# Routed attention and a bilinear feed-forward layer: weights rounded in pairs of chunks through one raw room, and a sum reloaded in front of the last down product

## The chip, the cores and the metric

One core of a Trainium2 chip. The time is the device time of one execution in microseconds (us), the median of several runs; less is better.

## The reference

```python
q_assign = argmax(q_n @ c_n, -1); k_assign = argmax(k_n @ c_n, -1)    # 16 clusters
mask = q_assign[..., :, None] == k_assign[..., None, :]
scores = where(mask, q @ k.T / sqrt(64), -1e9)
x = softmax(scores) @ v            # B=4, H=8, S=768, D=64; x becomes (3072, 512)
out = ((x @ w_a) * (x @ w_b)) @ w_out    # w_a, w_b: 512 x 1536, w_out: 1536 x 512, fp32
```

A query attends only to the keys of its own cluster. The three weights come as float64.

## The kernel before, in words

The sixteen pairs of heads of the four batches are worked one after the other. The first five are **dense**: scores of blocks of S x S (L599, keys of another cluster masked by a product of one-hot rows), exponentials on ACT (L612), products with v (L641), sums of the exponentials on DVE (`acc`, L630), denominators (L661), and a normalisation on DVE into `xT` (L681 to L694). The other eleven are **sorted**: rows are put into buckets of clusters by indirect DMAs of POOL (L1518), reloaded from DRAM (L1548 into `sq` and `sk`, L1552 into `v`), turned (L1561), scored and multiplied with v inside their buckets only (L1584 to L1619), normalised (L1629), kept (L1641) and fetched back in token order (L1652). The preparation of a sorted pair assigns clusters and counts places on DVE: copies L1384 (ACT) and L1408, then L1413 to L1506.

As soon as a batch's `xT` is ready, its feed-forward pieces follow on PE (helper line L734 for all their matmuls). Batch 0 does its ups plainly, in two halves of tokens (`ffn_block`: a product with w_a copied to `ha` at L787, a product with w_b multiplied into `h` at L791). Batches 1 to 3 use a scheme of seven products for ups (`ffn_ups`) and downs (`ffn_downs`, L1068 adds the products into `ha`, `rest` and `comb`, from which L761 stores the output). The sums of weights S1 to S4 that `ffn_ups` needs are computed in batch 1, kept in DRAM (`up_sums`) and reloaded later (L871 for S1 to S3, L880 for S4). S1's slot is `comb`, the same room that a down product's result lies in until it is stored.

**The weights.** float64 is rounded to fp32 by hand, in 36 chunks of 128 x 512. `load_w` (L306) brings a chunk of 512 KB of 8-byte words into one of two rooms `raw`. `round_w` does five DVE operations right behind each other (L317, L320, L324, L327, L335; `rest` is a room of its own) and a test of the exponents on ACT (L331, L332). Chunks 0 to 7 stand in fixed groups of the dense stage; the others come when `next_round` sees DVE idle by the planner's clock, or on demand: `up` rounds what its column block still lacks before it issues its product, w_a and w_b alternately.

**What sets the order.** The program is written out by a planner that keeps a clock per engine, runs each pair's chain of steps when its condition holds and fills PE with feed-forward pieces. Every engine executes its instructions in the order written; SP issues nearly all the DMAs, also in order, and stands at a DMA whose inputs are not there.

Of the kernel before, what the change touches and what calls it, by code (L numbers as in the profile page):

```python
# [157 lines left out]
def short_path(nc, tc, ctx, c, cn, centroids_in, casts, n_far, q, k, v,  # L158
# [20 lines left out]
    V, Vs, Vc, Vh, Vm, Vl, Vd, Vd_ = (Clocked(nc.vector, "V", us, *state)  # L179
                                      for us in (0.56, 0.19, 0.29, 0.44, 0.7, 0.83, 0.96, 0.42))  # L180
    S_, Ss, Sl = (Clocked(nc.scalar, "S", us, *state) for us in (0.5, 0.3, 0.85))
    Gi = Clocked(nc.gpsimd, "G", 1.28, *state)
    Qs = Clocked(nc.scalar, "S", 0.1, *state)
    Q_, Qr, Qc = (Clocked(nc.sync, "P", us, *state) for us in (0.42, 0.62, 2.0))
# [111 lines left out]
    def weight_room(i):  # L296
        if not deep or (i - deep[0]) % 4 > 1:
            return rawp.tile([P, WN], INT64, name="raw")
        at_ = (i - deep[0]) % 4 * 2 * WN
        return R_["wide"][:, at_:at_ + 2 * WN].bitcast(INT64)  # L300

    def load_w(i):
        if i >= len(w_parts):
            return
        raw = weight_room(i)
        Q_.dma_start(out=raw, in_=w_parts[i][1])  # L306
        raws[i] = raw

    def round_w(i):
        w = w_parts[i][0]  # L310
        wi = w.bitcast(INT32)
        raw = raws.pop(i)
        halves = lambda dt: raw.bitcast(dt).rearrange("p (n two) -> p n two", two=2)
        lo, hi = halves(UINT32)[:, :, 0], halves(INT32)[:, :, 1]


        Vh.tensor_scalar(out=wi, in0=hi, scalar1=3, scalar2=0x3FFFFFF8,  # L317
                                op0=ALU.logical_shift_left,
                                op1=ALU.bitwise_and)
        Vm.scalar_tensor_tensor(out=wi, in0=hi, scalar=SIGN_TOP, in1=wi,  # L320
                                       op0=ALU.bitwise_and, op1=ALU.bitwise_or)
# [5 lines left out]
        Vm.scalar_tensor_tensor(out=rest, in0=lo, scalar=2.0 ** -52,  # L327
                                       in1=rest, op0=ALU.mult, op1=ALU.mult)

        size = sizep.tile([P, WN], FP32, name="size")  # L330
        S_.activation(out=size, in_=halves(FP32)[:, :, 1], func=AF.Abs)  # L331
        S_.activation(out=size, in_=size, func=AF.Relu, scale=-STEEP,  # L332
                      bias=steep[:, 0:1],
                      accum_out=stat[:, 4 * NPAIR + i:4 * NPAIR + i + 1])
        V.tensor_tensor(out=w, in0=w, in1=rest, op=ALU.add)  # L335
# [421 lines left out]

    def store_next():
# [49 lines left out]
    def room():  # L808
        if not W:
            W["raw"] = [rawp.tile([P, 2 * WN], FP32, name="raw") for _ in range(2)]  # L810
            W["size"] = [sizep.tile([P, WN], FP32, name="size") for _ in range(2)]
# [27 lines left out]
    def ffn_ups(b, h):  # L839
# [158 lines left out]
        return pieces, both(*parts[0][0][1:3])  # L998
# [223 lines left out]
    def late_room():  # L1222
# [13 lines left out]
        R_.update(sq=sq, sk=sk, sqT=sqT, skT=sq, O=sqT, v=new(20 * (D + 1)))  # L1236
# [5 lines left out]
        loaded(deep[0] + 1)  # L1242
# [1006 lines left out]
```

## Time and profile before

| | |
|---|---|
| median of 3 runs | 936.36 us (936.02 to 937.34) |
| the profiled execution | 936.02 us |
| its span, first to last instruction | 934.2 us |
| mean granted clock of TensorE | 0.997 |
| PE busy | 916.4 us (98%) |
| DVE busy | 595.6 us (64%) |
| ACT busy | 252.1 us (27%) |
| POOL busy | 403.6 us (43%) |

The profiled execution's own time is its span and 1.8 us around it. The span holds matmuls from about 1 us to 928 us. Shares are means over the whole program; DVE's 64% is far from even, as the windows below show.

### The profile page before, as it was taken

The numbers are of one execution on the slowest core, as the hardware profiler recorded it, in microseconds if no ns is written. First come the engines' busy times: TensorE is split into PE (matmuls) and PEld (weight loads), VectorE is DVE, ScalarE is ACT, GpSimd is POOL, SyncE is SP. The second block draws the span as 40 slices with busy tenths as digits, with TensorE's granted clock in tenths as the row PEclk, the third lists the DMA queues.
The fourth block names the chain that finished last, engine by engine and source line by source line (L and its number), as shares of the span: only waits on it lengthen the run. The fifth ranks groups of instructions, "written<-read, shape, count | busy, mean of one in ns | idle before, by whom it ended". The sixth has DMA issues, their size and how long they took to land.

```text
span 934.2 us, 20904 instructions
## 1 busy us (share of the span) xinstructions
PE 916.4 (98%) x8145; PEld 488.6 (52%) x8145; DVE 595.6 (64%) x1253; ACT 252.1 (27%) x549; POOL 403.6 (43%) x407
## 2 busy tenths in 40 slices
PE   8999999899999999999999998999999999999997
PEld 5454444345455666545455664545455664444564
DVE  5888999688879776584757666563535343343532
ACT  5876656235332110222221100212221002111100
POOL 1027777554646656566656645666644000000000
PEclk9999999999999999999999999999999999999999
DMA  7978696689997958847939649663734011111310
GB/s 200 235 176 219 164 253 180 194 199 234 220 179 127 271 124 176 191 105 140 214 88 197 192 99 198 134 140 89 146 75 129 32 57 46 41 46 50 110 35 31
DMA packets 289610, 134.05 MB, mean 143 GB/s; under 512 B 242080, under 2 KB 270112, under 8 KB 289504
## 3 DMA queue, kind: packets, MB, share of 16 engines
q1 hardware_dynamic: 276288, 114.77, 52.9%
q0 software_dynamic: 12672, 17.39, 7.0%
q8 instruction: 66, 1.08, 0.5%
q10 hardware_dynamic: 544, 0.48, 0.2%
q14 instruction: 40, 0.33, 0.1%
HBM read 87.31 MB, written 45.17 MB: 142 GB/s over the span
## 4 chain that ended last, share of the span: by engine, by line
PE 89%; DVE 3%; DMA 3%; issue 1%; ACT 1%; SPq 1%; POOL 1%; POOLq 0%; DVEq 0%
PE m L734 68%; PE s L599 4%; PE O L641 3%; PE s L1584 3%; PE s L1610 2%; PE s L1619 2%; PE m L661 1%; PE O L1390 1%; PE s L1667 1%; DMA out_dram<-comb 1%; DMA kvd<-xT 1%; PE m L1379 1%; PE m L411 1%; DMA kvd<-whole,idx 1%; PE m L395 0%
## 5 line engine op out<-in xcount | busy, mean ns | idle before, releaser
L1652 POOL DMA_INDIRECT xT<-od,idx x132 | 129.7, 983 | 80.6 <-PE m L734 50.3
L734 PE MATMUL m<-xT,wa_sb 128*64 128x384 f32 x672 | 118.4, 494 | 1.1 <-DVE xT L694 1.1
L734 PE MATMUL m<-xT,wb_sb 128*64 128x384 f32 x672 | 116.7, 488 | 2.3 <-DVE wb_sb L335 2.3
L924 DVE TENSOR_TENSOR ha<-ha,m 128x384 f32<-128x384 f32 x72 | 39.6, 550 | 93.8 <-PE m L734 74.4
L1518 POOL DMA_INDIRECT qd<-whole,idx x72 | 72.8, 1011 | 56.7 <-PE m L734 24.1
L1518 POOL DMA_INDIRECT kvd<-whole,idx x72 | 71.3, 990 | 50.2 <-PE m L734 23.3
L921 ACT COPY h<-m 128x384 f32<-128x384 f32 x72 | 34.4, 478 | 210.5 <-PE m L734 203.5
L734 PE MATMUL m<-wo_sb,h 128*64 128x256 f32 x768 | 87.2, 380 | 0.0
L924 DVE TENSOR_TENSOR h<-h,m 128x384 f32<-128x384 f32 x72 | 39.6, 551 | 65.8 <-PE m L734 46.1
L734 PE MATMUL m<-raw 128*64 128x384 f32 x432 | 79.2, 487 | 0.2 <-DVE raw L873 0.2
L734 PEld LDWEIGHTS m<-xT,wb_sb 128*64 128x64 f32 x672 | 47.2, 137 | 60.5 <-issue 53.1
L734 PEld LDWEIGHTS m<-xT,wa_sb 128*64 128x64 f32 x672 | 47.7, 138 | 59.3 <-issue 52.6
L734 PEld LDWEIGHTS m<-wo_sb,h 128*64 128x64 f32 x768 | 54.5, 137 | 28.4 <-issue 1.9
L734 PE MATMUL m<-xT,h 128*64 128x256 f32 x576 | 64.7, 380 | 0.0
L1518 POOL DMA_INDIRECT qd<-wo_sb,idx x24 | 25.5, 1060 | 70.4 <-DVE wo_sb L1483 59.7
L734 PE MATMUL m<-xT,size 128*64 128x384 f32 x288 | 52.9, 488 | 0.0
L734 PEld LDWEIGHTS m<-xT,h 128*64 128x64 f32 x576 | 41.0, 137 | 20.6 <-issue 0.2
L734 PEld LDWEIGHTS m<-raw 128*64 128x64 f32 x432 | 30.8, 137 | 37.4 <-issue 35.0
L1518 POOL DMA_INDIRECT qd<-h,idx x36 | 39.0, 1084 | 26.1 <-DMA raw<-in_moe_w_out_dram 11.2
L921 ACT COPY ha<-m 128x384 f32<-128x384 f32 x54 | 25.8, 478 | 88.3 <-PE m L734 84.6
L1518 POOL DMA_INDIRECT kvd<-h,idx x36 | 37.7, 1047 | 15.7 <-issue 4.0
L599 PE MATMUL s<-qkT 64*128 64x384 f32 x240 | 43.7, 483 | 0.0
(262 smaller groups left out, 1497.1 us busy)
## 6 DMA issues: line engine op xcount, KB each, us to landing
whole<-kvd SPq DMA_DIRECT2D x44, 162.5 KB
whole<-qd SPq DMA_DIRECT2D x44, 160.0 KB
whole<-kvd SPq DMA_DIRECT2D x44, 160.0 KB
od<-whole SPq DMA_DIRECT2D x44, 160.0 KB
kvd<-xT SPq DMA_DIRECT2D x20, 322.5 KB
raw<-in_moe_w_a_dram SPq DMA_DIRECT2D x10, 512.0 KB
raw<-in_moe_w_b_dram SPq DMA_DIRECT2D x10, 512.0 KB
raw<-up_sums SPq DMA_DIRECT2D x38, 128.0 KB
```

The lines of the kernel that those rows point to most:

```text
L411: nc.tensor.matmul(out=ps[32 * kq:32 * kq + 32, 0:HB], lhsT=cTb[:, hp, :], rhs=qkTs[p][:, kq * HB:(kq + 1) * HB], start=True, stop=True)
L599: ins = nc.tensor.matmul(out=s[:, a, 0:HB], lhsT=Ts[p][r, S + j * P:S + (j + 1) * P], rhs=Ts[p][r, hf * HB:(hf + 1) * HB], start=start, st ...
L641: ins = nc.tensor.matmul(out=O_of[0][a * D:(a + 1) * D, 0:HB], lhsT=vs[p][:, a, j, :], rhs=probs[u][:, a, :], start=(j == 0), stop=(j == N ...
L661: nc.tensor.matmul(out=ps[a * D:(a + 1) * D, 0:HB], lhsT=ones, rhs=t[:, a, :], start=(n == 0), stop=(n == len(terms) - 1))
L734: ins = nc.tensor.matmul(out=ps[half], lhsT=lhsT[:, half], rhs=rhs, **kw)
L921: S_.copy(out=box[name], in_=box["X"][:, 0:HB])
L924: V.tensor_tensor(out=box[name], in0=box[name], in1=box[bank][:, 0:HB], op=ALU.add)
L1518: ins = Gi.indirect_dma_start(out=dst[:, 0:width], out_offset=bass.IndirectOffsetOnAxis(ap=M["idx"][:, w, j, a:a + 1], axis=0), in_=src, i ...
L1584: noted(nc.tensor.matmul(out=tiles[s // 2][r0:r0 + m, s % 2, c0:c0 + m], lhsT=M["skT"][r, h, 32 * x:32 * x + m], rhs=M["sqT"][r, h, 32 * x ...
L1610: noted(nc.tensor.matmul(out=ps[:, s, 65 * i:65 * i + 65], lhsT=pt[:, P * i:P * i + P], rhs=vt[:, i, :], start=True, stop=True))
L1619: noted(nc.tensor.matmul(out=ps[r, s, 65 * (2 + i):65 * (3 + i)], lhsT=pt[r, 2 * P + D * i:2 * P + D * i + D], rhs=vt[r, 2 + i, :], start= ...
L1652: paced(Gi.indirect_dma_start(out=M["xs"][:, j, a * D:(a + 1) * D], out_offset=None, in_=od[n][:, :], in_offset=bass.IndirectOffsetOnAxis( ...
```

## The change

1. **Weights in pairs of chunks.** There are 18 parts of 128 x 2 x 512, loaded by one DMA of 1 MB each. In the dense stage there is one room `raw`, so part i+1 is loaded 1.0 us (planner's clock) after part i's last operation; later it alternates with the room `wide`. `rest` no longer has a room: operation three writes it over the high words of `raw`, with a stride of two, and four and five work on it there. Each of the five operations is issued singly by `next_round`, 1.25 to 1.5 us apart or later, between other work. The first operation of a part, and the test on ACT that is issued with it, wait until 8.0 us (parts 0 to 5) or 6.0 us after the planned issue of its load.
2. **S1 of a first unit.** Before the last down product of a batch, the pending stores are issued up to that of `comb`, and S1 is loaded into `comb` behind it. Before, this load stood with the first up product of the next batch.
3. **Results over v.** A sorted pair's normalised result goes over its own `v`. The turns therefore no longer wait for the last pair's keep; the reload of `v` (4 and 5) does, in a chain of its own with the masking.

```diff
     def weight_room(i):
-        if not deep or (i - deep[0]) % 4 > 1:
-            return rawp.tile([P, WN], INT64, name="raw")
-        at_ = (i - deep[0]) % 4 * 2 * WN
-        return R_["wide"][:, at_:at_ + 2 * WN].bitcast(INT64)
+        if not deep or (i - deep[0]) % 2:
+            return rawp.tile([P, 2, WN], INT64, name="raw")
+        return R_["wide"][:, 0:4 * WN].bitcast(INT64).rearrange("p (c n) -> p c n", c=2)
...
-        rest = wtp.tile([P, WN], FP32, name="rest")
-        Vh.tensor_scalar(out=rest.bitcast(INT32), in0=wi,
-                                scalar1=SIGN_EXP, scalar2=None,
-                                op0=ALU.bitwise_and)
...
+        rest = halves(FP32)[:, :, :, 1]
+
+        def check():
+            size = sizep.tile([P, 2 * WN], FP32, name="size")
+            flat = size.rearrange("p (c n) -> p c n", c=2)
+            Sw.activation(out=flat, in_=rest, func=AF.Abs)
+            Sw.activation(out=size, in_=size, func=AF.Relu, scale=-STEEP,
+                          bias=steep[:, 0:1],
+                          accum_out=stat[:, 4 * NPAIR + i:4 * NPAIR + i + 1])
+
+        return [
+            lambda: (check(), Vm.tensor_scalar(
+                out=wi, in0=hi, scalar1=3, scalar2=0x3FFFFFF8,
+                op0=ALU.logical_shift_left, op1=ALU.bitwise_and)),
+            lambda: Vw.scalar_tensor_tensor(
+                out=wi, in0=hi, scalar=SIGN_TOP, in1=wi,
+                op0=ALU.bitwise_and, op1=ALU.bitwise_or),
+            lambda: Vm.tensor_scalar(
+                out=hi, in0=wi, scalar1=SIGN_EXP, scalar2=None, op0=ALU.bitwise_and),
+            lambda: Vw.scalar_tensor_tensor(
+                out=rest, in0=lo, scalar=2.0 ** -52, in1=rest,
+                op0=ALU.mult, op1=ALU.mult),
+            lambda: Vw.tensor_tensor(out=w, in0=w, in1=rest, op=ALU.add)]
...
         def up(w_sb, f):
-            while rounds and rounds[0] < 8 * (f // 4) + 8:
-                round_one(rounds.pop(0))
+            round_until(4 * (f // 4) + 4)
...
             if n == 0:
-                now_ = combinations if b == 1 else (combinations[0], combinations[3])
-                ps[0] = both(*now_, ps[0])
+                ps[0] = both(*(combinations if b == 1 else combinations[3:]), ps[0])
...
-                M["O"] = R_["O"].rearrange("p (s i d) -> p s i d", s=4, d=D)
+                M["O"] = M["v"][:, :, :, 0:D]
...
-        chain += row(FREE, -9.0, turns[0:2], "A",
-                     lambda: was("keep", n - 1, 4) and was("sqs", n, 4.5))
+                  plan(FREE, 0, lambda: run_chain(
+                      [plan(FREE, 0, lambda: reload(4), lambda: was("keep", n - 1, 3.5), "R"),
+                       plan(FREE, 1.6, lambda: reload(5), kind="R")]
+                      + row(FREE, 0, masking, "A", lambda: was("reload", n, 4.0))
+                      + [plan(FREE, 0, lambda: mark("masks", n))], now[0] + 1.6, start, n))]
+        chain += row(FREE, -9.0, turns[0:2], "A", lambda: was("sqs", n, 4.5))
...
         if b > 1:
             ffn.insert(first + 1, (0, ahead))
+            ffn.insert(max(0, len(ffn) - 1), (0, lambda: (stored(W["comb"]), last_in())))
...
+    def round_step():
+        doing.popleft()()
+        if not doing:
+            i = at_round[0]
+            if deep:
+                loaded(i + 2)
+            else:
+                at(last[0] + 1.0, lambda t: loaded(i + 1))
...
     def next_round(t):
-        if not rounds:
+        if not rounds and not doing:
             return
-        i = rounds[0]
-        if not (i in raws and arrived[i] + (7.5 if i < 12 else 4.5 if i < 22 else 6.5) <= now[0] and may_round(i)):
+        if not doing:
+            i = rounds[0]
+            if not (i in raws and arrived[i] + (8.0 if i < 6 else 6.0) <= now[0]
+                    and may_round(i)):
+                at(now[0] + 0.5, next_round)
+                return
+            begin_round()
+        elif not may_round(at_round[0]):
             at(now[0] + 0.5, next_round)
             return
-        rounds.pop(0)
         begin()
-        round_one(i)
-        at(max(t + (4.2 if deep else 3.5), now[0]), next_round)
-
-    at(98.0, next_round)
+        round_step()
+        at(max(t + (1.5 if deep else 1.25), now[0] - 2.0), next_round)
+
+    at(START, next_round)
```

PE's matmuls are the same 8145, in another order. The order at three places, each row a line, an operation and its tiles (a line of the change is 1 to 6 higher than before):

**DVE, around the cluster copies of a sorted pair's preparation (`wo_sb`), before:**

```order
L317 TENSOR_SCALAR wa_sb<-raw 128x512
L320 SCALAR_TENSOR_TENSOR wa_sb<-raw,wa_sb 128x512
L324 TENSOR_SCALAR rest<-wa_sb 128x512
L327 SCALAR_TENSOR_TENSOR rest<-raw,rest 128x512
L335 TENSOR_TENSOR wa_sb<-wa_sb,rest 128x512
L317 TENSOR_SCALAR wb_sb<-raw 128x512
L320 SCALAR_TENSOR_TENSOR wb_sb<-raw,wb_sb 128x512
L324 TENSOR_SCALAR rest<-wb_sb 128x512
L327 SCALAR_TENSOR_TENSOR rest<-raw,rest 128x512
L335 TENSOR_TENSOR wb_sb<-wb_sb,rest 128x512
L630 TENSOR_TENSOR acc<-pt 128x768
L1408 STREAM_TRANSPOSE wo_sb<-m 128x384
```

**and the same copy (now L1413) in the change:**

```order
L1491 TENSOR_SCALAR wo_sb<-wo_sb 128x32
L1493 SCALAR_TENSOR_TENSOR wo_sb<-wo_sb 128x32
L1495 TENSOR_REDUCE stat<-wo_sb 128x1
L325 TENSOR_SCALAR wb_sb<-raw 128x2x512
L328 SCALAR_TENSOR_TENSOR wb_sb<-raw,wb_sb 128x2x512
L1413 STREAM_TRANSPOSE wo_sb<-m 128x384
L331 TENSOR_SCALAR raw<-wb_sb 128x1024
L333 SCALAR_TENSOR_TENSOR raw<-raw 128x1024
L336 TENSOR_TENSOR wb_sb<-wb_sb,raw 128x2x512
```

Two whole chunks and a sum stood ahead of the copy; two operations of one part stand there now. A few rows further up, the normalisation L681 to L694 of a block of `xT` stood behind L1506, L1475 and L1480 of the sorted pair; now it (L682 to L695) stands ahead of them.

**DVE, the last chunk of w_b's second column block (f = 4 to 7), before:**

```order
L791 TENSOR_TENSOR h<-ha,m 128x384
L1452 TENSOR_REDUCE wo_sb<-wo_sb 128x32
L1454 TENSOR_REDUCE stat<-wo_sb 128x2
L1456 SCALAR_TENSOR_TENSOR wo_sb<-wo_sb,rank 128x32
L1496 TENSOR_TENSOR wo_sb<-wo_sb 128x512
L1499 TENSOR_REDUCE wo_sb<-wo_sb 128x32
```

(six operations of 128x32 on `wo_sb`, L1462 to L1471, follow)

```order
L1471 SCALAR_TENSOR_TENSOR wo_sb<-wo_sb 128x32
L317 TENSOR_SCALAR wb_sb<-raw 128x512
L320 SCALAR_TENSOR_TENSOR wb_sb<-raw,wb_sb 128x512
L324 TENSOR_SCALAR rest<-wb_sb 128x512
L327 SCALAR_TENSOR_TENSOR rest<-raw,rest 128x512
L335 TENSOR_TENSOR wb_sb<-wb_sb,rest 128x512
L791 TENSOR_TENSOR h<-ha,m 128x384
```

**and the part that holds it (part 7) in the change:**

```order
L333 SCALAR_TENSOR_TENSOR raw<-raw 128x1024
L1457 TENSOR_REDUCE wo_sb<-wo_sb 128x32
L1459 TENSOR_REDUCE stat<-wo_sb 128x2
L1461 SCALAR_TENSOR_TENSOR wo_sb<-wo_sb,rank 128x32
L1501 TENSOR_TENSOR wo_sb<-wo_sb 128x512
L336 TENSOR_TENSOR wb_sb<-wb_sb,raw 128x2x512
L1504 TENSOR_REDUCE wo_sb<-wo_sb 128x32
L795 TENSOR_TENSOR h<-ha,m 128x384
L1467 CAST wo_sb<-wo_sb 128x32
```

Both times the last rounding operation stands ahead of the product of f = 4 (the second L791, the second of whose operands it makes). Before, the five stood behind eleven operations of the sorted pair and behind the product of f = 3; now the first three stand 11 to 13 rows up, ahead of f = 3's product, the fourth behind that, and the six operations of 128x32 behind the last.

**SP, the boundary of batches 1 and 2, before:**

```order
L761 DMA out_dram<-rest 128x256
L871 DMA raw<-up_sums_187 128x256 x2
L1548 DMA whole<-kvd_212 32x20x64 x2
L761 DMA out_dram<-comb 128x256
L1552 DMA whole<-kvd_212 128x5x65 x2
L871 DMA comb<-up_sums_187 128x256
L880 DMA size<-up_sums_187 128x128 x2
```

**and in the change:**

```order
L766 DMA out_dram<-rest 128x256
L877 DMA raw<-up_sums_187 128x256 x2
L1553 DMA whole<-qd_217 32x20x64 x2
L766 DMA out_dram<-comb 128x256
L877 DMA comb<-up_sums_187 128x256
L1352 DMA whole<-in_k_dram 32x24x32 x4
L886 DMA size<-up_sums_187 128x128 x2
```

The reload of S1 now stands right behind the store of `comb`; four loads of a sorted pair's keys and S4's reload stand behind it.

## Rows read from the trace of the kernel before

**Rows 1.** The page, part 1: busy time, share of the span, instructions.

```profile
PE 916.4 (98%) x8145; PEld 488.6 (52%) x8145; DVE 595.6 (64%) x1253; ACT 252.1 (27%) x549; POOL 403.6 (43%) x407
```

**Rows 2.** Waits of PE: who waited for whom: total us, times, longest.

```profile
PE m L734 <- DMA comb<-up_sums: 2.9, 1, 2.9
PE m L734 <- DVE wb_sb L335: 2.3, 1, 2.3
PE m L734 <- DVE xT L694: 1.1, 1, 1.1
...
PE m L661 <- DVE wo_sb L1408: 0.8, 1, 0.8
...
PE m L661 <- ACT wo_sb L1384: 0.7, 1, 0.7
```

**Rows 3.** Timeline 174:185: start, us, engine, line, operation, count, idle before and releaser.

```profile
176.10 0.19 DVE L1471 SCALAR_TENSOR_TENSOR wo_sb<-wo_sb 128x32 f32<-128x32 int32 x1
176.21 0.42 DVE L317 TENSOR_SCALAR wb_sb<-raw 128x512 int32<-128x512 int32 x1
...
178.65 0.69 DVE L335 TENSOR_TENSOR wb_sb<-wb_sb,rest 128x512 f32<-128x512 f32 x1
...
179.40 0.87 PE L734 MATMUL m<-xT,wb_sb 128*64 128x384 f32 x4 [2.34 <-DVE wb_sb L335]
...
180.09 4.44 PE L734 MATMUL m<-xT,wa_sb 128*64 128x384 f32 x16
```

**Rows 4.** Windows: stretch, us, busy of PE, PEld, DVE, ACT, POOL, PEclk, DMA share, GB/s.

```profile
45.00:50.00 5.00, 5.00 (x50) 2.42 (x50) 1.97 (x3) 3.11 (x7) 0.00 (x0) 1.00 1.03 284
124.00:150.00 26.00, 24.88 (x167) 10.95 (x169) 24.90 (x51) 14.04 (x30) 19.37 (x18) 1.00 0.92 250
180.00:185.00 5.00, 5.00 (x22) 1.92 (x20) 2.38 (x6) 0.42 (x2) 1.91 (x2) 0.66 0.89 335
```

**Rows 5.** Timeline of PE at the boundary of batches 1 and 2.

```profile
571.42 2.75 PE L734 MATMUL m<-xT,wa_sb 128*64 128x384 f32 x16
...
578.31 1.51 PE L734 MATMUL m<-xT,comb 128*64 128x384 f32 x8 [2.85 <-DMA comb<-up_sums]
```

**Rows 6.** Timeline of DVE, the last subtraction into comb.

```profile
566.46 0.42 DVE L1068 TENSOR_TENSOR comb<-comb,m 128x256 f32<-128x256 f32 x1 [0.85 <-PE m L734]
```

**Rows 7.** Timeline of SP's queue in the same stretch.

```profile
570.05 1.80 SPq L761 DMA_DIRECT2D out_dram<-comb  x1
571.89 2.04 SPq L1552 DMA_DIRECT2D whole<-kvd  x2
576.02 0.34 SPq L871 DMA_DIRECT2D comb<-up_sums  x1
```

**Rows 8.** Chain of waits, 560:582: start, us, what.

```profile
570.05 5.91 DMA out_dram<-comb
...
576.02 2.15 DMA comb<-up_sums
```

**Rows 9.** Groups of DVE instructions by form: count, busy us, mean ns, idle before.

```profile
L327 DVE SCALAR_TENSOR_TENSOR rest<-raw,rest 128x512 f32<-128x512 uint32 x26 | 18.1, 698 | 0.9
...
L630 DVE TENSOR_TENSOR acc<-acc,pt 128x768 f32<-128x768 f32 x24 | 22.9, 955 | 1.4
...
L1068 DVE TENSOR_TENSOR comb<-comb,m 128x256 f32<-128x256 f32 x36 | 14.9, 414 | 4.2 <-PE m L734 4.2
...
L317 DVE TENSOR_SCALAR wb_sb<-raw 128x512 int32<-128x512 int32 x10 | 4.4, 445 | 0.0
```

**Rows 10.** Groups of ACT instructions by form, same columns.

```profile
L332 ACT ACTIVATE size<-size,steep 128x512 f32<-128x512 f32 x36 | 26.0, 722 | 1.2
...
L331 ACT ACTIVATE size<-raw 128x512 f32<-128x512 f32 x26 | 17.9, 687 | 1.8 <-DMA raw<-in_moe_w_a_dram 1.0 <-DMA raw<-in_moe_w_b_dram 0.7
```

**Rows 11.** Timeline of SP: one weight load's issue.

```profile
144.64 0.37 SPq L306 DMA_DIRECT2D raw<-in_moe_w_a_dram  x1
```

**Rows 12.** Timeline of ACT: the instruction that waited for that load.

```profile
149.93 0.69 ACT L331 ACTIVATE size<-raw 128x512 f32<-128x512 f32 x1 [1.02 <-DMA raw<-in_moe_w_a_dram]
```

More of the change, by code (lines that the diff above doesn't have):

```diff
@@ L304, in load_w @@
             return
-        raw = weight_room(i)
-        Q_.dma_start(out=raw, in_=w_parts[i][1])
-        raws[i] = raw
+        raws[i] = weight_room(i)
+        Qw.dma_start(out=raws[i], in_=w_parts[i][1])
     def round_w(i):
@@ L332, in round_w @@
[L332 to L335, printed above, removed]
+        halves = lambda dt: raw.bitcast(dt).rearrange(
+            "p c (n two) -> p c n two", two=2)
+        lo, hi = halves(UINT32)[:, :, :, 0], halves(INT32)[:, :, :, 1]
+        rest = halves(FP32)[:, :, :, 1]
[6 more added lines that the diff above has]
+                          accum_out=stat[:, 4 * NPAIR + i:4 * NPAIR + i + 1])
@@ L756, in sum_next, with stored @@
             Q_.dma_start(out=to, in_=x)
+    def stored(room_):
+        while any(y.tensor is room_.tensor for _, y in stores):
+            store_next()
     def store_next():
@@ L997, in ffn_ups @@
             pieces += [(2 * HB, f) for f in ps]
-        return pieces, both(*parts[0][0][1:3])
+        return pieces, parts[0][0][0], both(*parts[0][0][1:3])
     FREE_XT, FREE_ROOM = 4, 2
@@ L1691, in may_load @@
             return bool(is_late) and was("put", n - 2, 1) and not (
-                rounds and n == EARLY + 2)
+                (rounds or doing) and n == EARLY + 2)
         free = lambda: "P" not in busy and was("sims", n - 1)
@@ L1723, in sorted_pair @@
                   plan(FREE, 1.6, lambda: reload(2),
[L1724 to L1727 removed]
+                       lambda: was("values", n - 1, 0.3), "R"),
+                  plan(FREE, 1.6, lambda: reload(3), kind="R"),
+                  plan(FREE, 0, lambda: run_chain(
[4 more added lines that the diff above has]
+        chain += row(FREE, -9.0, turns[0:2], "A", lambda: was("sqs", n, 4.5))
         chain += row(FREE, 0, turns[2:4], "A", lambda: was("sks", n, 4.5))
[L1729 removed]
         chain += [plan(FREE, 1.8, lambda: scores(False), lambda: "T" not in busy, "T"),
                   plan(FREE, 0.2, lambda: scores(True), kind="T"),
[L1732 removed]
+                  plan(FREE, 0.6, lambda: (values(0), values(1)),
+                       lambda: was("masks", n, 0.5), "T"),
                   plan(FREE, 1.2, keep, kind="R")]
@@ L1802, in short_path @@
     credit = 0
-    due = {g: [i] for i, g in enumerate((1, 3, 4, 6, 11, 17, 20, 22))}
     START, PERIOD = 15.5, 4.2
     STARTS = [0.0, 76.0, 104.0, 140.0, 150.0] + [190.0] * NPAIR
-    rounds = []
+    rounds = list(range(len(w_parts)))
+    doing, at_round = deque(), [0]
     def loaded(i):
@@ L1815, in loaded @@
             load_w(done_to[0])
-            arrived[done_to[0]] = max(clocks["P"], clocks["V"] if done_to[0] > 21 else now[0])
-    done_to = [1]
-    arrived = {}
-    def round_one(i):
-        loaded(i)
-        round_w(i)
-        if deep:
-            loaded(i + 4)
-        elif i < 20:
-            at(last[0] + 2.5, lambda t: loaded(i + 2))
-        else:
-            loaded(i + 2)
-    rounds.extend(range(8, len(w_parts)))
+            arrived[done_to[0]] = max(clocks["P"], now[0])
+    done_to = [0]
@@ L1833, in may_round @@
     def may_round(i):
-        idle = clocks["V"] <= now[0] + 0.6
-        if i < 16:
-            return idle or now[0] > 124 + 6.5 * (i - 8) and clocks["V"] <= now[0] + 2.0
-        if i < 24:
+        idle = clocks["V"] <= now[0] + 1.0
+        if i < 8:
+            return clocks["V"] <= now[0] + (2.0 if now[0] > 18 + 15 * i else 0.6)
+        if i < 12:
             return idle or bool(is_late)
         return clocks["V"] <= now[0] + 1.4 and (
-            was("after", EARLY, 4) if i < 31 else was("put", EARLY - 1, 2))
+            was("after", EARLY, 4) if i < 15 else was("put", EARLY - 1, 2))
@@ L2002, in weight_parts @@
 def weight_parts(c, w_a, w_b, w_out):
-    n_ch, n_f, wide = c["wa_sb"].shape[1], c["wa_sb"].shape[2], 512
-    parts = [(sb[:, ch, n:n + wide], src[ch * P:(ch + 1) * P, n:n + wide])
-             for n in range(0, n_f, wide) for ch in range(n_ch)
+    n_f, wide = c["wa_sb"].shape[2], 512
+    rows = lambda src, ch: src[ch * P:(ch + 2) * P].rearrange("(c p) n -> p c n", p=P)
+    parts = [(sb[:, ch:ch + 2, n:n + wide], rows(src, ch)[:, :, n:n + wide])
+             for n in range(0, n_f, wide) for ch in (0, 2)
              for sb, src in ((c["wa_sb"], w_a), (c["wb_sb"], w_b))]
-    return parts + [(c["wo_sb"][:, f, :], w_out[f * P:(f + 1) * P, :])
-                    for f in (5, 6, 7, 8, 9, 10, 11, 0, 1, 2, 3, 4)]
+    return parts + [(c["wo_sb"][:, f:f + 2, :], rows(w_out, f))
+                    for f in (6, 8, 10, 4, 2, 0)]
 def small_weights(nc, tc, c, w_a, w_b, w_out):
```

63 lines of the change are left out of this document (26 added, 37 removed).

## The prediction

> **What bounds the kernel now.** I read the page's busy times first: PE is busy for 98% of the span [rows 1], so a change of order alone can win little more than PE's waits. The second view is PE's list of waits [rows 2]: two large ones of different causes, 2.9 us for S1's reload (`comb` from `up_sums`) and 2.3 us for a rounded piece of w_b, and small ones of 0.7 to 1.1 us from the dense stage, where DVE is busy for 24.90 of 26 us [rows 4]. Then the timeline and the clock around each of the two. At 176.21 the chunk's first operation starts right behind L1471, the end of a block of the sorted pair's work, its last ends at 178.65 + 0.69 = 179.34, and PE goes on at 179.40 after 2.34 us [rows 3]. The next sixteen matmuls take 4.44 us [rows 3], against 2.75 us for sixteen of the same shape elsewhere [rows 5]; the granted clock of 180 to 185 us is 0.66 [rows 4], so a part of that stretch ran at the lower of the two levels, 1.2 GHz instead of 2.4, behind an idle PE. The idle time cost 4.44 - 2.75 = 1.69 us more than itself. The wait for S1, though longer (2.85 us), had no such sequel: its eight matmuls took 1.51 us [rows 5], about half of 2.75.
>
> **The chunk on demand (L335, f = 4).** The change rounds the same weights earlier, one operation at a time: in the written order the part's operations stand between other work, the last ahead of six operations behind which the chunk stood. I take the wait off completely, **-2.34**, and with it the clock's fall, **-1.69**. Bounds: if only the rounding moved and the block stayed long, 0 to half of it would be left; 0 and -4.03 are the ends.
>
> **DVE's work.** The sums come from forms of other sizes: a two-input operation takes 414 ns at 256 elements, 698 at 512, 955 at 768 [rows 9], about 1.0 ns for each further element, so 1024 elements take an estimated 1.22 us; a one-input TENSOR_SCALAR takes 445 ns at 512 [rows 9] and, with the same fixed part of some 0.15, an estimated 0.73 at 1024. A chunk costs 2 x 0.445 + 3 x 0.70 = 2.99 us, 36 of them 107.6; a part 2 x 0.73 + 3 x 1.22 = 5.12, 18 of them 92.2. That frees 15.4 us of DVE, 16 x 2.99 - 8 x 5.12 = 6.9 of it ahead of f = 4. By itself it shortens nothing, since PE is the bound; it matters where PE waits for DVE. I set it at nothing beyond the waits named here; were DVE's work to grow instead, its cover is gone in the dense stage, where 1.1 us of 26 is free [rows 4].
>
> **The small waits for DVE.** L1408 stood behind ten rounding operations in a row; two (and half as many sums) stand there now, so its 0.8 us of PE [rows 2] should go. The normalisation that PE waited 1.1 us for (L694 [rows 2]) stood behind some 1.3 us of a sorted pair's operations and now stands ahead of them. I take both, **-1.9**; the ends are 0 (another operation is late in their place) and -2.6, with the 0.7 behind L1384 [rows 2] gone too.
>
> **S1.** The last subtraction into `comb` ends at 566.46 + 0.42 = 566.88 [rows 6]. The store is issued only at 570.05, the reloads of v follow, and S1's load is issued at 576.02, as soon as the store has landed [rows 7]: 5.91 us from issue to landing, then 2.15 for S1 [rows 8]. PE wanted it at 578.31 - 2.85 = 575.46 [rows 5]. If SP reaches the store at 566.9, S1 is there at 566.9 + 5.91 + 2.15 = 575.0, just in time; each microsecond that SP is late beyond 0.5 comes back as a wait. In the new order fewer issues stand ahead of the store since a block of four key loads has moved behind it, but one pair of reloads is still there (a pair took about 1 to 2 us, L1552 2.04 [rows 7]). I take 0.5 us as what is left: **-2.35**, ends 0 (SP reaches the store at 570.05 as before) and -2.85. What waits now is SP: it stands at S1's load until the store has landed, with four key loads and S4's reload queued behind it, up to 5.9 us. S4 is used some four products later (about 4 x 1.5 us [rows 5] after S1), and the keys belong to a sorted pair for which PE has other pieces; I set that at nothing, up to 1 us.
>
> **Loads of 1 MB into one room.** Before, a load of 0.5 MB was issued at 144.64 [rows 11] and the ACT instruction that waited for it started at 149.93 [rows 12]: 5.29 us. Another 0.5 MB at the 250 GB/s of 124 to 150 us [rows 4] is 2.1 us, so I estimate 7.4 us. The code allows 8.0 for parts 0 to 5 and 6.0 for 6 and 7, so those two could be 1.4 us late each. Both ACT and DVE stand then, with exponentials behind them. Before, ACT waited 1.8 us in all for weights [rows 10], and one PE wait of 0.7 us, behind L1384, came of it [rows 2, 12]: 0.4 us of PE for each of ACT. 2.8 x 0.4 = 1.1. The test on ACT comes in one piece twice as large: 0.69 + 0.72 [rows 10] become at most 2.8 us, half as often. For both I add **+1.0**, ends 0 and +3.
>
> **The sorted pairs.** Results over v, masks in a chain of their own and the new order of w_out's chunks move DVE and SP work of sorted pairs. No wait for scores, values or turns stands among PE's large ones [rows 2]; feed-forward pieces cover them. I cost this at nothing; without that cover it would be one more wait of about 1 us for each of some pairs.
>
> **Sum.** -2.34 - 1.69 - 1.9 - 2.35 + 1.0 = -7.3. Against the profiled execution (936.02: its span of 934.2 and 1.8 around it) that is 928.7; the median of the runs, 936.36, is 0.34 above it, so I predict **929.0**.
>
> **Rival one: S1 only changes what it waits for.** If SP is as busy in front of the store as before, the chain 570.05 + 5.91 + 2.15 ends at 578.1, where PE waited until 578.31. Then 929.0 + 2.35 = 931.4. For it: 5.91 us from issue to landing is long for 128 KB, the DMA engines were full. Against: the order has fewer issues ahead. Chance 0.18.
>
> **Rival two: operation three loses its speed.** A TENSOR_SCALAR of 512 takes 445 ns with a strided source [rows 9], less than two thirds of the 698 of a two-input operation; with a strided destination no row shows it. If it took the two-input 1.22 us, a part would cost 0.5 more, 18 parts 9 us of DVE, 4 of them in the dense stage, which has little to spare [rows 4]. With half to all of it on PE: 931 to 933. The Trainium skill, page "VectorE: DVE Perf Modes", section "What auto-detection actually checks", asks for a single source and destination in SBUF with even (or equal) outermost dimensions, not for unit stride; by it the operation keeps its speed and this rival falls. I follow the rows on the source side and give it 0.10.
>
> **Rival three, the slower side: one room is too few.** With two rooms a load lay beside the rounding of the chunk before. With one, every part waits for its own load, and ACT and DVE, in order, stand in front of it with the exponentials that PE needs. If a 1 MB load takes twice the 5.29 us, 10.6, parts 1 to 5 are 2.6 us late and 6 and 7 4.6 us: 22 us of ACT waiting. With ACT's wait of 1.02 [rows 12] giving 0.7 of PE [rows 2], that is 0.67 x 22 = 14.8 us, and 929.0 - 1.0 + 14.8 = 942.8. It decides from about 9.2 us a load: 5 x 1.2 + 2 x 3.2 = 12.4 us of waits at 0.67 undo the 8.3 us gained. For it: the DMA engines are full in places (share 1.03 in 45 to 50 us, 0.92 in 124 to 150 [rows 4]); against it: 284 and 335 GB/s move 1 MB in 3 to 4 us [rows 4]. The Trainium skill, page "Trainium Kernel Development and Optimization", section "Best Practices", says to double-buffer so that DMA overlaps with compute; by it this change goes the wrong way, and this rival is what that rule makes of it here. The trace of before bears the rule out only in part: the two rooms still let ACT wait [rows 12]. Chance 0.24, spread over 934 to 943: 0.13 of it slower, 0.11 no change.
>
> That the parts are still rounded on demand (the change does not do what it says) I leave out: the order shows them spread.
>
> **How the numbers follow.** Main case 0.48, rival one 0.18, rival two 0.10, rival three 0.24. A measurement of this kernel tells about 0.2%, 1.9 us, from no change. The first three are all faster by more, 0.76; same 0.11; slower 0.13. The main case runs from 925.8 (all of S1's wait, the waits for L1384 and of the loads gone, 929.0 - 0.5 - 0.7 - 1.0, and 1 us of smaller ones) to 931. The range takes in rivals one and two and the near part of three, to 935.5.
>
> **What would show it.** Right: PE's list has no wait for `wb_sb` of the rounding, no stretch near 180 us with a granted clock below 1, and a wait for S1 under 1 us with its load issued near 573; the first and third rounding operation at 0.7 us, the others at 1.2; DVE busy near 580. Wrong: PE waiting for `pt` or `acc` behind an ACT that waits for raw weights, loads of 9 us and more, operation three at 1.2 us, or S1's wait still at 2 to 3 us with its store issued as late as before. The prediction fails as a whole if new waits in the dense stage add up to over 6 us.

## The result

The changed kernel takes **947.29 us** (945.76 to 949.14, 4 runs) against 936.85 us of the kernel before on the same chip (936.02 to 937.83, 4 runs): ratio 1.0112, 95% interval 1.0094 to 1.013. It is 10.4 us slower; 929.0 was forecast. Its profiled execution took 947.9 us, 11.9 more than the one of before.

The page's first line for the changed kernel: PE is busy for longer in the same matmuls, which the clock below explains.

```profile
PE 922.6 (98%) x8145; PEld 490.2 (52%) x8145; DVE 580.0 (61%) x1163; ACT 243.5 (26%) x495; POOL 417.6 (44%) x407
```

PE's list of waits in the changed kernel (total us, times, longest):

```profile
PE s L600 <- ACT pt L613: 3.9, 6, 1.3
PE s L1589 <- issue: 2.9, 1, 2.9
PE m L662 <- ACT wo_sb L1440: 2.5, 1, 2.5
PE m L396 <- ACT qkT L404: 1.9, 1, 1.9
...
PE s L1589 <- DVE whole L1566: 0.9, 1, 0.9
PE s L600 <- ACT xT L613: 0.8, 1, 0.8
PE m L735 <- DVE comb L879: 0.8, 2, 0.4
...
PE m L662 <- ACT wo_sb L1389: 0.7, 1, 0.7
```

The four waits that the prediction named [rows 2] are gone: `wb_sb` (2.3), S1's `comb` from `up_sums` (2.9; L879 is another), `xT` (1.1) and L1408 (0.8), 7.1 us together, and the half clock behind the first, 1.7. In their place stand 8.4 us behind exponentials and copies of ACT (3.9 + 2.5 + 1.9 + 0.8 for L613, L1440 and L404, less some 0.7 that L612 had before), 0.8 for `comb` behind DVE's L879, 3.8 us at the scores L1589, and three falls of the clock. The first of ACT's longer waits in the timeline, ACT and then PE:

```profile
39.10 1.15 ACT L319 ACTIVATE size<-raw 128x1024 f32<-128x1024 f32 x1
40.28 1.15 ACT L320 ACTIVATE size<-size,steep 128x1024 f32<-128x1024 f32 x1
41.33 0.18 ACT L320 ACTIVATION_READ_ACCUMULATOR size<-size,steep 128x1 f32 x1
41.42 1.05 ACT L404 COPY qkT<-m 128x512 f32<-128x512 f32 x2
```

```profile
39.54 0.60 PE L1384 MATMUL m<-ident,wo_sb 128*128 128x128 f32 x4
42.04 0.66 PE L396 MATMUL m<-ident,qk 128*128 128x128 f32 x4 [1.90 <-ACT qkT L404]
...
42.97 2.40 PE L600 MATMUL s<-qkT 64*128 64x384 f32 x8
```

The test of one part of the weights (L319, L320 and the read of its sum) holds ACT from 39.10 to 41.42. The copy of `qkT` behind it (L404) is what PE's transposes wait for, 1.90 us, and the eight score matmuls after it take 2.40 us where the eight at 35.78 take 1.45. A whole test stands in the same way in ACT's order ahead of the other longer waits: it starts at 63.84, 93.30, 117.53 and 169.28 us, and PE goes on at 67.71, 97.18, 120.74 and 172.19 (the test of 117.53 had itself waited 2.28 us for a load of `ohT`). The windows show the clock there and at the two other places (columns as in [rows 4]):

```profile
40.00:45.00 5.00, 3.10 (x18) 1.51 (x16) 3.95 (x5) 4.23 (x8) 0.00 (x0) 0.83 0.47 134
45.00:50.00 5.00, 5.00 (x30) 1.91 (x28) 1.89 (x2) 2.24 (x5) 0.00 (x0) 0.83 1.03 259
172.00:177.00 5.00, 4.82 (x20) 1.99 (x22) 1.95 (x4) 0.91 (x5) 1.57 (x3) 0.66 0.08 25
240.00:245.00 5.00, 5.00 (x40) 1.90 (x38) 0.81 (x2) 0.08 (x1) 3.78 (x5) 1.00 1.26 213
250.00:255.00 5.00, 2.26 (x32) 2.00 (x32) 4.10 (x6) 0.00 (x0) 0.56 (x1) 0.65 0.51 106
255.00:260.00 5.00, 5.00 (x68) 2.17 (x72) 2.27 (x4) 0.02 (x1) 0.95 (x1) 0.66 0.97 289
```

A granted clock of 0.83 or 0.66 over 5 us is 1.7 or 3.4 us at the lower level, 1.2 GHz, and costs half of that as far as PE is busy in it: 1.7 us near 43 (two windows of 0.83), 1.7 near 173, and about 3.0 from 251 to 258 (6.9 us at the lower level, less the 0.9 in which PE waited). That is 6.4 us against 1.7 before. Sum: -7.1 - 1.7 + 8.4 + 0.8 + 3.8 + 6.4 = +10.6 of the 11.9.

The durations came out as estimated (DVE, then ACT; columns as in [rows 9]):

```profile
L333 DVE SCALAR_TENSOR_TENSOR raw<-raw 128x1024 f32<-128x1024 uint32 x13 | 15.9, 1223 | 0.2
...
L331 DVE TENSOR_SCALAR raw<-wa_sb 128x1024 int32<-128x1024 int32 x6 | 4.4, 726 | 1.3 <-ACT size L319 1.0
L325 DVE TENSOR_SCALAR wa_sb<-raw 128x1024 int32<-128x1024 int32 x6 | 4.3, 713 | 0.1
```

```profile
L320 ACT ACTIVATE size<-size,steep 128x1024 f32<-128x1024 f32 x18 | 20.7, 1150 | 0.6
...
L319 ACT ACTIVATE size<-raw 128x1024 f32<-128x1024 f32 x13 | 15.2, 1168 | 2.3 <-DMA ohT<-h 2.3
```

1.22 us for the two-input operations, 0.72 for the one-input ones, with the strided destination (L331) too; a test is 1.17 + 1.15 + 0.19 = 2.5 us in one piece, where it was 0.69 + 0.72 + 0.19 = 1.6 [rows 10]. DVE's busy time fell from 595.6 to 580.0 us, by the 15 us worked out.

At the boundary of batches 1 and 2, SP's queue now:

```profile
581.94 0.36 SPq L766 DMA_DIRECT2D out_dram<-comb  x1
586.22 0.34 SPq L877 DMA_DIRECT2D comb<-up_sums  x1
```

The store of `comb` is issued as soon as `comb` is there (581.91), S1's load follows 4.3 us after it instead of 6.0 [rows 7], and PE does not wait for S1.

The place near 250 us, SP, DVE and PE:

```profile
231.54 1.90 SPq L305 DMA_DIRECT2D whole<-in_moe_w_out_dram  x1
...
234.84 4.35 SPq L1553 DMA_DIRECT2D whole<-qd  x2
...
241.14 3.96 SPq L1646 DMA_DIRECT2D od<-whole  x4
245.19 1.51 SPq L1553 DMA_DIRECT2D whole<-kvd  x2
```

```profile
244.19 1.57 DVE L1566 STREAM_TRANSPOSE whole<-whole 128x640 f32<-128x640 f32 x2 [4.56 <-DMA whole<-qd]
...
250.90 0.84 DVE L1566 STREAM_TRANSPOSE whole<-whole 128x640 f32<-128x640 f32 x1 [4.70 <-issue]
```

```profile
251.85 0.92 PE L1589 MATMUL s<-whole 32*128 32x128 f32 x8 [2.92 <-issue]
253.66 2.35 PE L1589 MATMUL s<-whole 32*128 32x128 f32 x56 [0.89 <-DVE whole L1566]
```

The reload of a sorted pair's q (L1553, `whole<-qd`) is issued for 4.35 us behind a 1 MB load of w_out, and DVE's turn L1566, already next in its order, stands 4.56 us for it. For the next 4.70 the profile names no releaser ("issue"); k is the likely one, since SP issues its second half only behind the keep of the pair before (L1646). In 240 to 245 us DVE is busy for 0.81 us, with the DMA engines full (share 1.26, above). PE comes to the scores L1589 and waits 2.92 and 0.89 us.

### The profile page after: what moved, and what is told of

Its sections match the earlier page's. It is cut to its first block, busy times and chain, and to the rows that moved or that the text cites. A ratio compares the mean times of both kernels' runs of the same rounds, so it can differ in the third digit from the quotient of the medians.

```text
span 946.2 us, 20737 instructions
## 1 busy us (share of the span) xinstructions
PE 922.6 (98%) x8145; PEld 490.2 (52%) x8145; DVE 580.0 (61%) x1163; ACT 243.5 (26%) x495; POOL 417.6 (44%) x407
## 4 chain that ended last, share of the span: by engine, by line
PE 89%; DMA 3%; ACT 3%; DVE 2%; issue 1%; SPq 1%; ACTq 0%; DVEq 0%
PE m L735 68%; PE s L600 4%; PE O L642 3%; PE s L1589 3%; PE s L1615 2%; PE s L1624 2%; DMA whole<-kvd 1%; PE m L662 1%; PE s L1672 1%; ACT pt L613 1%; PE O L1395 1%; PE m L1384 1%; ACT size L319 1%; DMA out_dram<-comb 0%; DVE whole L1566 0%
## 5 line engine op out<-in xcount | busy, mean ns | idle before, releaser
L1657 POOL DMA_INDIRECT xT<-od,idx x132 | 136.8, 1036 | 92.8 <-PE m L735 60.7
L1523 POOL DMA_INDIRECT qd<-wo_sb,idx x24 | 27.5, 1146 | 73.6 <-DVE wa_sb L325 64.1
L1523 POOL DMA_INDIRECT qd<-h,idx x36 | 39.2, 1088 | 34.4 <-DMA whole<-in_q_dram 17.8
L1523 POOL DMA_INDIRECT kvd<-h,idx x36 | 42.6, 1182 | 15.5 <-issue 5.8
L1566 DVE STREAM_TRANSPOSE whole<-whole 128x640 f32<-128x640 f32 x44 | 35.4, 826 | 17.5 <-DMA whole<-kvd 8.2
```

The costliest lines, as they stand in the source:

```text
L1523: ins = Gi.indirect_dma_start(out=dst[:, 0:width], out_offset=bass.IndirectOffsetOnAxis(ap=M["idx"][:, w, j, a:a + 1], axis=0), in_=src, i ...
L1566: Vl.transpose(out=M[t][:, h], in_=M[s][:, :, 32 * h:32 * h + 32])
L1657: paced(Gi.indirect_dma_start(out=M["xs"][:, j, a * D:(a + 1) * D], out_offset=None, in_=od[n][:, :], in_offset=bass.IndirectOffsetOnAxis( ...
```

## The experiments

All but `b_short` and `b_ct_short` ran on chips on which the kernel before itself takes 971 to 978 us; each ratio is to runs of before on its own chip. On those chips the change costs 0.7% (`after_again`, below), not 1.1%, so what an edit gives back there is read against 0.7%. "Same order" means that the instructions of all engines but the one named keep their order.

**1. The test of the weights on ACT.** Three edits of the changed kernel and its repetition.

`a_no_test` leaves out both operations:

```diff
-            Sw.activation(out=flat, in_=rest, func=AF.Abs)
-            Sw.activation(out=size, in_=size, func=AF.Relu, ...)
```

> The changed kernel without the test of the weights' exponents on ACT (both operations of each of the 18 parts left out; the computed output does not use them), every other engine's order unchanged. Theory A (the test, 2.5 us of ACT in one piece, holds back exponentials and copies that PE needs): the PE waits behind L613, L404 and L1440 of the changed kernel (3.9 + 0.8 + 1.9 + 2.5 = 9.1 us) and the two stretches at half clock near 43 and 173 us (2 x 1.7) go, 947.3 becomes 936 (934.5 to 939); the waits at L1589 near 250 us stay. Rival (loads into the one room, or the order of DVE, make PE wait): 946 to 948, the waits stay under other names.

`a_test_split` issues the second operation with operation four (the line of the edit that does it):

```diff
-            lambda: Vw.scalar_tensor_tensor(
+            lambda: (check_end(), Vw.scalar_tensor_tensor(
                 out=rest, in0=lo, scalar=2.0 ** -52, in1=rest,
```

> The changed kernel with the test in two pieces: Abs with operation one as before, Relu and its sum only with operation four, so that other ACT work gets in between; every other engine's order unchanged. Theory A: pieces of 1.15 and 1.35 us instead of 2.5 leave PE under 3 us of waits behind ACT and no fall of the clock before 200 us: 938 (936 to 941). Rival (it is ACT's total work, not the length of the piece): 945 to 948.

`after_again` is the changed kernel, unedited.

> The changed kernel itself once more, on the chip of this comparison, so that the others have it beside them. If chips only differ in their level: 1.011 of before (1.007 to 1.015). If the chip of the second comparison, where before takes 972, weighs the waits otherwise: under 1.005, and then the differences found there have to be read against this run alone.

| run | ratio to before | 95% interval |
|---|---|---|
| after_again | 1.0071 | 1.0040 to 1.0103 |
| a_no_test | 1.0010 | 0.9988 to 1.0032 |
| a_test_split | 0.9991 | 0.9969 to 1.0014 |

Taking the test out, or only apart, brings 0.6 to 0.8%, with PE, DVE, SP and POOL in the same order: theory A held, and it is the piece that counts, not ACT's work, which the split keeps. (`after_again` itself lies between the two cases that were expected.) A second pair shows the same: `a_turns_back` and `a_split_turns` (part 4) differ in ACT's order alone, and the split takes 1.0103 to 1.0033. In the first pair the whole test ran on one chip and the split on another, in the second pair the other way round, so the chip does not make the difference. On a chip of the faster kind no such edit was run; there the 8.4 us of waits and the clock behind two of them are read from the trace. PE's waits of after_again and of a_test_split (whose lines are 6 higher):

```profile
PE s L600 <- ACT pt L613: 6.2, 7, 3.2
PE m L662 <- ACT wo_sb L1440: 3.6, 1, 3.6
...
PE m L396 <- ACT qkT L404: 1.9, 1, 1.9
...
PE m L662 <- ACT wo_sb L1389: 1.5, 1, 1.5
```

```profile
PE m L668 <- ACT wo_sb L1395: 1.8, 1, 1.8
PE s L606 <- ACT pt L619: 1.5, 2, 1.2
...
PE m L402 <- ACT qkT L410: 0.6, 1, 0.6
PE m L668 <- ACT wo_sb L1446: 0.6, 1, 0.6
```

Not all of ACT's waits go. The one for the copy L1389 (L1395 in the split) stays, and `a_no_test`, which has no test at all, still waits 4.1 us behind exponentials, 3.35 of them near 96 us, where after_again waits 3.18 near 99. In `a_no_test` the wait for L1440 is down to 0.6 us and the 1.9 for L404 is gone.

`b_test_twice` lengthens the piece in the kernel before, the two operations done twice in a row, same order:

```diff
+        nc.scalar.activation(out=size, in_=halves(FP32)[:, :, 1], func=AF.Abs)
+        nc.scalar.activation(out=size, in_=size, func=AF.Relu, ...)
         S_.activation(out=size, in_=halves(FP32)[:, :, 1], func=AF.Abs)
```

> The kernel before with the test of each chunk done twice on ACT, one right behind the other (3.2 us in one piece instead of 1.6, 36 times; no other engine's order changes). Theory A (a long piece of ACT in front of exponentials and copies makes PE wait): 16 pieces in the dense stage, each up to 1.6 us later, PE waits behind L612, L1384 and L403 grow by 8 to 14 us in all: 1.012 of before (1.007 to 1.018). Rival (in the changed kernel it was the place in the new order, not the length): under 1.004.

Measured 1.0138 (1.0105 to 1.0171), and the waits behind L612 (here L616) and L1384 (here L1388) are the largest of ACT's:

```profile
PE s L603 <- ACT pt L616: 8.7, 6, 3.1
PE m L665 <- ACT wo_sb L1388: 2.8, 1, 2.8
```

`b_short` goes the other way in the kernel before: the second operation is issued some 1.2 us later.

```diff
+        at(last[0] + 1.2, lambda t: nc.scalar.activation(
+            out=size, in_=size, func=AF.Relu, ...))
```

> The kernel before with the test's second operation (Relu and sum) issued on ACT some 1.2 us of the planner's clock later than the first, so that other ACT work gets between; no other engine's order changes. Theory A: PE waits behind exponentials shrink by 2 to 4 us: 0.996 to 0.998 of before. Rival (a piece of 1.6 us is short enough to be covered): 0.999 to 1.002.

Measured 1.0003 (0.999 to 1.0015): the rival. In 17 of the 26 tests that read `raw`, other ACT work does get between the two operations. A piece of 1.6 us was covered on this chip, one of the faster kind; 2.5 and 3.2 us are not on the slower ones.

`a_split4_late` cut the test into four pieces of 512 elements, one with each of four operations, and planned turns later (below).

> As the run before, with the test in four pieces of 512 elements (Abs of one chunk with operation one, of the other with two, Relu and sum with four and five), planned at their own durations; 0.7 us more ACT work a part. Theory A: no PE wait behind the test is left, the ratio is 0.002 to 0.004 under that of the run before. Rival (ACT's work, not its pieces): the same or higher by 0.002.

Measured 1.0121 (1.0081 to 1.0161), the worst of the splits: with other costs in the planner the whole order changed, and a part of w_b was rounded late again (PE waited 6.6 us for `wb_sb`). It says nothing on the pieces.

**2. S1's load.** `b_s1` is the kernel before with S1's move alone, two SP rows:

```diff
+            ffn.insert(max(0, len(ffn) - 1), (0, lambda: (stored(W["comb"]), last_in())))
```

> The kernel before with the move of S1 alone (two rows of SP change places, all other engines' orders unchanged). Theory (the prediction's term): S1's wait of 2.85 us shrinks to 0.5, 936.5 becomes 934.2 (933.5 to 934.8). Rival (SP reaches the store no earlier, so S1 lands when it did): 936.0 to 936.9, the wait stays at 2 to 3 us.

Measured 0.9988 (0.9962 to 1.0014), and PE still waits 2.9 us. `b_turns` (below) has no such edit and PE waits 0.7 us. SP's rows of the two, b_s1 first:

```profile
600.86 0.65 SPq L765 DMA_DIRECT2D out_dram<-comb  x1
607.26 0.34 SPq L875 DMA_DIRECT2D comb<-up_sums  x1
```

```profile
598.52 0.36 SPq L761 DMA_DIRECT2D out_dram<-comb  x1
...
603.29 0.45 SPq L871 DMA_DIRECT2D comb<-up_sums  x1
```

In b_s1 the store is issued 2.7 us after `comb` is ready (597.75 + 0.42 = 598.17), behind two loads of sums and two reloads of a sorted pair, and S1's load follows 6.4 us after it; in b_turns the store is issued at once. `a_split_nos1` undoes the move in the changed kernel with the split test:

> The changed kernel with the test split, and S1's move undone (S1 is loaded with the first up product again). If the move itself brings the gain there: a wait of PE for comb of 2 to 3 us comes back at the boundary of batches 1 and 2, the ratio rises from 0.999 to 1.0015 (1.000 to 1.004). Rival (the other order of the sorted pairs had freed SP, so S1 comes in time either way): no such wait over 1 us, 0.997 to 1.001.

No PE wait for `comb` behind a reload is in its list: the rival held on the mechanism. The ratio, 1.0026 (1.0009 to 1.0044), is above that of a_test_split all the same. Its list has 3.0 us more behind exponentials (L619, 4.5 for 1.5), but at 85 and 97 us, where the two programs are the same; they ran on different chips, and whether the difference is S1's stays open. `a_weights_split` (part 5) has neither S1's move nor results over v, and there too the store is issued as soon as `comb` is ready (605.08), and PE does not wait for S1:

```profile
605.11 0.36 SPq L772 DMA_DIRECT2D out_dram<-comb  x1
```

So each of the other two parts of the change alone makes SP's queue reach the store early. Moved one product earlier, ahead of a pair of reloads, the move does work: `b_chunk_s1`, with the early chunk of the next point.

> The run before, and S1 moved as in the change but one product earlier, so that SP reaches the store of comb before a pair of reloads of the sorted pair. If SP's queue is what made S1 late in the run with S1's move alone: S1's wait falls from 2.9 to under 1 us and the ratio by another 0.002 to 0.003, to 0.993 (0.991 to 0.996). Rival (the landing takes as long whenever it is issued, since the DMA engines are full): S1's wait stays over 2 us, the ratio that of the run before.

Measured 0.9941 (0.9919 to 0.9962), PE's wait for S1 1.1 us.

**3. The chunk at f = 4.** `b_chunk` rounds it ahead of f = 3's product in the kernel before:

```diff
-            while rounds and rounds[0] < 8 * (f // 4) + 8:
+            while rounds and rounds[0] < (16 if f == 3 and w_sb is wb_sb else 8 * (f // 4) + 8):
```

> The kernel before with one thing moved: the last chunk of w_b's second column block is rounded in front of the product of f = 3 (five DVE operations move up 12 places, four SP rows change places, PE, ACT and POOL keep their order). This is the prediction's term of -2.34 - 1.69 by itself. If it holds: no PE wait for wb_sb, no half clock behind it, and 4.0 us less: 0.9958 of before (0.994 to 0.998). Rival (DVE or the sorted pair's steps behind it become the wait): 0.999 to 1.002.

Measured 0.9980 (0.9958 to 1.0002): half of what was expected. PE has no wait for `wb_sb`, but stands for 1.15 us ahead of the next matmuls with w_b (184.57); the profile names no releaser. They start as f = 3's product on DVE ends (183.97 + 0.55 us), behind the rounding that the edit put ahead of it.

**4. The sorted pairs.** `b_turns` is results over v alone, on the kernel before (the diff of the change's third part).

> The kernel before with results over v alone (turns no longer wait for the last pair's keep; reloads of v and masks in a chain of their own). Theory B (turns written ahead of their reloads make DVE and then PE's scores wait): waits of PE at the scores of 2 us or more in one or two places between 220 and 420 us, often with half a clock behind, ratio 1.005 (1.002 to 1.009). Rival (the wait near 250 us comes of the weights' loads and roundings in DVE's and SP's order there, not of the turns): 0.998 to 1.002, no such wait.

Measured 0.9960 (0.9936 to 0.9985): it is faster, against theory B; S1's wait is the gain that its list shows. `a_turns_back` undoes it in the changed kernel, `a_split_turns` in that with the split test, `a_split_late` keeps it and plans the turns later (`was("sqs", n, 9.0)` for 4.5, and so for k).

> The changed kernel with the results over v undone (their own room again, the turns wait for the last pair's keep, reloads and masks in the chain). Theory B (the turns and scores of a sorted pair are now written earlier than their reloads land, and PE stands at L1589 near 250 us for 2.9 + 0.9 us and at half clock behind it for 6.8, which costs 3.4): 7.2 us less, 940 (938.5 to 942), no wait over 0.5 us at the scores L1589. Rival (the reloads are late because SP's queue is full of the 1 MB loads and stores, so the wait only moves): 946 to 948.

> The changed kernel with the test split as in the second run and the results over v undone as in the third; only ACT's order differs from that third run. Theory A: the split takes about 1.0% off a kernel with either order of the sorted pairs: 1.010 becomes 1.000 (0.996 to 1.004). Theory B (early turns cost 0.7%) would give 0.992, with the split and the turns both gained. Rival to A (the split helped only through one lucky place): over 1.006.

> The changed kernel with the split test, and the turns planned 9.0 us behind the planned issue of their reloads in place of 4.5. Theory B: PE's 2.9 and 0.9 us at the scores near 250 us and the half clock behind them go, and the ratio falls from 0.999 to 0.992 (0.989 to 0.996). Rival (that stall moves to another place, or what is planned later makes other steps late): 0.997 to 1.002.

Measured 1.0103 (1.0053 to 1.0154), 1.0033 (1.0009 to 1.0058) and 0.9992 (0.9968 to 1.0016). In all three the wait of 2.9 us near 250 is gone, and none got faster by it than its like (1.0071, 0.9991 and 0.9991). The wait needs early turns and the new weights together, since neither b_turns nor a_weights_split has a wait at the scores of more than 1.2 us. What it costs in the end stays open.

**5. The weights alone.** `a_weights_split` is the change's first part with the split test, the other two parts undone.

> The weights' part alone (pairs of chunks, one room, spread operations), with the test split; results over v and S1's move undone. If the spread rounding gains what the prediction said for it (the wait at f = 4 with its clock, 4 us), and nothing else is lost: 0.996 of before (0.993 to 0.999), with S1's wait of about 2.9 us still there or not as SP's order has it. Rival (the spread operations hold back the sorted pairs' preparation on DVE, so that PE waits behind oh_s and wo_sb between 130 and 180 us): 1.000 to 1.005.

Measured 1.0050 (1.0025 to 1.0076): the rival. PE's list has no `wb_sb`, but 2.0 us at L1402, 1.9 for `oh_s` and 1.5 for a copy of ACT, all between 130 and 175 us and with two falls of the clock. That these waits make up the 0.5% is read from the list, not tested. The parts add up within their intervals, each about 0.25% to either side: 0.50% for the weights with the split test, -0.40% for b_turns and -0.12% for b_s1 make -0.02% (a_test_split: -0.09%).

**6. What gains, put together on the kernel before.** `b_chunk_turns` is b_chunk and b_turns; `b_chunk_turns_s1b` adds S1 one product earlier.

> The kernel before with results over v and the early chunk (ten DVE and four SP rows differ from the run with results over v alone). If the two gains add, 0.4% and 0.2 to 0.4%: 0.993 (0.990 to 0.996), no PE wait for wb_sb and none over 1 us for comb. Rival (the early chunk's gain goes to the next wait of the dense stage): 0.996.

> The run before with S1 also moved in front of the last down product but one (12 or fewer SP rows differ). Results over v alone left only 0.7 us of S1's wait, so little is left to gain: 0.992 to 0.994, 0.000 to 0.001 under the run before. If S1's move and results over v hinder each other on SP: 0.001 to 0.003 above it.

Measured 0.9931 (0.9906 to 0.9956) and 0.9949 (0.9923 to 0.9975), not told apart. `b_ct_short` is the first with the test apart as in b_short:

> The kernel before with the early chunk, results over v, and the test taken apart as in the run before. Theory A: 0.001 to 0.004 under the 0.9931 measured for the two alone: 0.990 to 0.992. Rival: 0.993 to 0.995.

It ran with b_short on a chip where before takes 937.44 us: 932.69 us (931.03 to 934.59), 0.9954 (0.9938 to 0.9969), the one version measured faster than both kernels on such a chip. It is not under the 0.9931 of b_chunk_turns, as theory A had it, and the test apart gained nothing in b_short, so the gain should be that of the other two edits. Its windows where the kernel before stood and then ran at half clock [rows 3, 4], and its largest waits inside the program:

```profile
172.00:177.00 5.00, 5.00 (x34) 2.19 (x32) 4.71 (x14) 1.38 (x5) 3.40 (x4) 1.00 0.67 195
177.00:182.00 5.00, 5.00 (x34) 2.26 (x32) 2.57 (x7) 1.06 (x2) 3.35 (x4) 1.00 1.08 356
```

```profile
PE m L735 <- DMA comb<-up_sums: 1.8, 1, 1.8
PE m L735 <- DVE xT L695: 1.2, 1, 1.2
...
PE m L662 <- DVE wo_sb L1409: 1.0, 1, 1.0
```

PE is busy throughout at the full clock: the 2.34 us and the clock's fall behind them are both gone.

## Why the prediction was wrong

- **The step that failed** stands at the end of "Loads of 1 MB into one room": the test "comes in one piece twice as large", and "for both I add +1.0". The loads alone had come to 1.1 by then, so the test was put at nothing. Its length was right (2.5 us; at most 2.8 was said), its price was not: 8.4 us more of PE waits behind ACT and two falls of the clock, 3.4. Pieces of 1.6 us cost nothing on the faster kind of chip (b_short), and the step took twice the length to be as cheap; b_test_twice shows that 1.6 us more in each piece costs 1.4% on the slower kind, and the split shows that it is the piece that costs, not the work. The loads, for their part, cost nothing: in the dense stage ACT never stood for a weight load. The prediction's own sign of failing as a whole, new waits of over 6 us in the dense stage, came true.
- **How much of the miss that is.** From -7.3 forecast to +11.9 in the trace it is 19 us: 8.4 and 3.4 where 1.0 was added, 3.8 and 3.0 at the sorted pairs, 0.8 for `comb`, and some 1 us that the sum above does not find. With the split test the change is at 0.9991, not at the 0.992 that was forecast, so the test explains the slowdown and not the whole of the missing gain.
- **The new order of the rounding** was taken to cost nothing. By itself, with the split test, the weights' part is at 1.0050, where the gain at f = 4 was expected to make it 0.996.
- **The clock** appears in the sum as a gain only. A wait added can bring its own fall, at 1.7 us or more here; three did.
- **The sorted pairs** were costed at nothing, "feed-forward pieces cover them". The turns, early in DVE's order, stood for reloads behind a 1 MB load with the DMA engines full: 3.8 us of PE and about 3.0 of clock in the trace. No experiment gave them back: where this wait was gone, no kernel got faster by it.
- **The chunk on demand** (-2.34, -1.69) was right in the changed kernel's trace, and its clock in b_ct_short's. **The small waits** (-1.9) went too.
- **S1** went as forecast, -2.85 of which -2.35 was counted, but not by its move: results over v (b_turns) and the new weights (a_weights_split) each rearrange SP's queue so that the store goes out early. That the term came out is luck. Rival one described b_s1.
- **Rival three** had the right sign for another reason: ACT waited for a weight load once by more than 2 us (5.05, until 217.09, after the dense stage), and no PE wait followed. Its place, ACT in order ahead of the exponentials, was right; what stood there was work, not waiting. **Rival two** fell: L331 takes 0.73 us with its strided destination, as the Trainium skill, page "VectorE: DVE Perf Modes", section "What auto-detection actually checks", has it. The rule to double-buffer (the Trainium skill, page "Trainium Kernel Development and Optimization", section "Best Practices") forecast the sign, but one room as such cost no PE wait that the trace shows.

## What to carry to other kernels

An engine that is a quarter busy can still set the pace through the length of what it does in one go: before merging two operations, look at who stands behind them in that engine's order and how long that one's reader can wait. Price a possible wait of PE with the clock's fall behind it. When several small moves come together, measure each alone: here the part meant to take PE's waits away cost 0.5% even with the test split, and the one that looked like bookkeeping, results over v, was worth 0.4% by itself.

## What the runs showed of the hardware

Chips differ more than the change does: before takes 937 us on some and 971 to 978 on others (971.37 and 977.76 at two times on one of them). One form shows part of it, the kernel before on the first chip and b_s1, with the same order of PE, on a slower one:

```profile
L1584 PE MATMUL s<-whole 32*64 32x64 f32 x1056 | 17.8, 229 | 0.0
```

```profile
L1587 PE MATMUL s<-whole 32*64 32x64 f32 x1056 | 27.8, 235 | 9.8 <-issue 9.1
```

The small score matmuls, each about as long (229 and 235 ns), kept PE busy for 27.8 us instead of 17.8 and had 9.1 us of idle "issue" ahead of them. PE's list has 6.8 to 12.2 us of "issue" at these scores in every trace from a slower chip; on the faster ones it has none but the changed kernel's 2.9. And the same idle time does not always bring the lower clock: the 2.85 us before S1 were followed by full clock [rows 5], 3.0 us at the same place in b_short by a fall to half (granted clock 0.92 in 575 to 580 us and 0.74 in 580 to 585).
